# A list scheduler without program order between two readers of one tile: adaLN, an S4 convolution and a squared-ReLU FFN on one core

## The chip, the cores and the metric

The kernel runs on one core of one Trainium2 chip. The metric is the device time of one execution in microseconds (us), as the median of three runs. Five engines share the work: TensorE (PE, with its weight loads as PEld), VectorE (DVE), ScalarE (ACT), GpSimd (POOL) and SyncE (SP), which only issues transfers. The profile is of one execution, with all times counted from the start of its span.

## The reference

The input `u` is 2048 x 512, the state space model has 128 complex states for each of the 512 channels, the feed-forward part goes from 512 to 1792 and back. Cut to what is computed:

```
sa, ca, ga, sb, cb, gb = (silu(c) @ w_mod) split in six
h = layernorm(u) * (1 + ca) + sa
K[d, l] = Re sum_n C[d,n] * exp(dt[d] * A[d,n] * l) * dt[d] * B[d,n]
y = causal convolution of h with K along l (by FFT of 4096) + h * Dskip
x = u + ga * y
h = layernorm(x) * (1 + cb) + sb
out = x + gb * (relu(h @ w1 + b1)**2 @ w2 + b2)
```

## The kernel before

The kernel has four stages. In the head the parameters of the state space model are worked out (`parameters`, two calls: one for the first block of 64 channels, instructions of 128 x 64, one for the other seven, 128 x 7 x 64, lines 486 to 537), the modulation vectors (L579) are turned into a scale and a shift for every row (L611 to L616), and 16 rows of 128 positions are scaled (DVE L626 and L627), transposed by matmuls (PE L631, into two PSUM banks in turn) and copied (ACT L634).

The middle stage makes the convolution. Channels go in eight blocks `c` of 64. Each block passes through two matmul stages of a transform, stage 1 (PE L668, copied by ACT L670) and stage 2 (PE L678, copied by ACT L701), and a transfer that swaps its halves (L708). The transform of K is made in 32 units `u` of 16 channels, four to a block. For one unit POOL multiplies out amplitudes (L780, L784) from tables of exponentials (L754), and adds up the phases as integers (L736 for a block, L760 for a unit); ACT takes sine, absolute value and cosine (L770 to L772); DVE makes four products (L794 to L797); PE sums over the states (`kg`, L804), which ACT and DVE bring to the buffer `ksb` (L870, L871) for stage 1. K with a number means the L804 group of that unit, so K29 is the thirtieth. DVE multiplies the two spectra (L814), PE makes the first step of the inverse (L823), DVE copies it (L829).

The end of the convolution begins to load the feed-forward weights: w1 (L936) and w2 (L962) arrive in `work`, and ACT (L918) and DVE (L919) split each value into a high and a low part. A spread of gb (L912), the table `i2c` of the last inverse step (its transfer L903) and the rows of x once more (L907) belong here. Then come the second inverse step (PE L1009), the second layer norm (L1016 to L1046) and the FFN (L1083 to L1087 and L1125 to L1127), with the stores of the output.

What sets the order: all instructions are traced in program order, and then `keep_order` makes groups of them, finds for each group the groups that must come before it, and goes through them as a list scheduler, with one queue for each engine. Durations come from `weight`. Of the groups that are ready on an engine, the one with the longest way to the end is taken; `urgent` adds a number to that way for a whole block of code, taken from the table `HURRY`. The string table `ORDER` sets in which unit of K's loop which piece is traced: `r` a row, `A` to `H` the transform of a block, `a` to `h` its product and inverse, `0` to `7` its swap, `x` a batch of exponentials, `l` the late modulation. Matmuls of the FFN are held in program order by `in_turn`. The engine order that results is fixed by added dependences. In `before`, a group depends on an earlier one that touches the same cells of a tile, if either writes, or if the tile is a PSUM bank, or if both run on the same engine.

Of the kernel before, what the change touches and what calls it, by code (L numbers as in the profile page):

```python
# [13 lines left out]
I32 = mybir.dt.int32  # L14
# [23 lines left out]
NU = 32  # L38
EXPS = [(0, 1), (1, 1), (2, 2), (4, 2), (6, 2)]
ORDER = (  # L40
    "rrrrrrrrxrrrrrrrrABAA.CAAABABA.ClB.CBBCC0xC.BaaBCaaaaa.a.D..1bCDDbDbbE.E"
    "b2bE..DDExEbb.cDcccc.DE.F.FcE.c3EcFdxddFFdGF.dGdG..dd4.FeFeGee.HHeH.eH5G"
    ".e.HeGffGfHf.GH.ffH..6f.fgggg..g.gg7hhhhg"
).split(".")
HURRY = (-5134, -11930, -6, -54444, 14765, -82, 97968, -2, -603, 233, 1864, 6642, -284, 13749, 1407, -107, 6332, 4392, -789, 6471, 2150, -1844, 36197, -951, 83, -77, 1508, -2294, 89, -1791, -139, -157, 2431, -579, 674, -2630, -13726, -38198, -1676, -5575, -55525, 18242, 558, -2589, 11726, 2336, -215, -10792, 64542, -107, 672, 3536, -676, -860, 25428, 5010)
PIECES = "ABCDEFGHabcdefghl"


# [63 lines left out]
def weight(ins):  # L112

    out = ins.outs[0] if ins.outs and hasattr(ins.outs[0], "bass_ap") else None
    n = free_size(out) if out is not None else 1
    if "DMA" in type(ins).__name__:
        inside = not any("Dram" in type(a.bass_ap.tensor).__name__.title() for a in (*ins.ins, *ins.outs))
        return 60, n * out.ap[0][1] * 4 / (145 if inside else 330)
    match str(ins.engine).split(".")[-1]:
        case "PE":  # L120
            if len(ins.ins) < 2:
                return 10, 10
            cols, moving = free_size(ins.ins[1]), free_size(ins.ins[0])
# [12 lines left out]
            if n == 1:  # L136
                t = 200
            elif len(operands(ins.ins)) > 1:
                t += 95 if n > 128 else 140
            elif n <= 128:  # L140
                t += 26
            elif type(ins).__name__ == "InstTensorCopy" and n < 1024:
                t -= 40
        case "DVE":
            t = 70 + 1.04 * (free_size(ins.ins[0]) if type(ins).__name__ == "InstBNStats" else n)
            if n <= 4:
                t = 110
            elif len(operands(ins.ins)) > 2:
                t += 60
            elif type(ins).__name__ == "InstReciprocal":  # L150
                t = 70 + 6.3 * n
        case "Pool":
            t = 250 + 1.72 * n
        case _:
            t = 30
    return t, t + 65


def keep_order(tc, traced, slots, in_turn, whole, urgent):
# [40 lines left out]
    for g, il in enumerate(groups):  # L200
        for ins in il:
            for write, aps in ((False, ins.ins), (True, ins.outs)):
                for a in aps:
                    if getattr(a, "bass_ap", None) is None or "Dram" in type(a.bass_ap.tensor).__name__.title():
                        continue
                    name, rows, cells = region(a)
                    bank = name[:2] in ("ps", "tg", "kg")
                    slot = slots.get(name, name)
                    if slot in held and held[slot] != name:
                        left_by[name] = {x[0] for x in seen.get(held[slot], ())}  # L210
                    held[slot] = name
# [109 lines left out]
def tile_adaln_ssm_ffn(  # L321
# [18 lines left out]
    nc = tc.nc  # L340
# [220 lines left out]

    for c, n in ((1, 7),):
        mark = len(nc.cur_bb.bb.instructions)
        for _ in parameters(c, n):
            pass
        hurry(mark, HURRY[2])


    sl = ctile("sl", [P, 4])
# [53 lines left out]
    def row_pieces():  # L623
        for s, row in enumerate(rows):
            mark = len(nc.cur_bb.bb.instructions)
            nc.vector.scalar_tensor_tensor(row, row, mv1[:, s, 0:1], g1, op0=ALU.subtract, op1=ALU.mult)  # L626
            nc.vector.scalar_tensor_tensor(row, row, mv1[:, s, 1:2], s1, op0=ALU.mult, op1=ALU.add)  # L627
            ps = free_banks[s % 2]
            for g in range(4):
                for q in range(4):  # L630
                    nc.tensor.matmul(  # L631
                        ps[32 * q : 32 * q + 32, 128 * g : 128 * g + 128], ident[:, 32 * g : 32 * g + 32],
                        row[:, 128 * q : 128 * q + 128], start=True, stop=True)
            nc.scalar.copy(xj[:, :, 4 * s : 4 * s + 4], ps.rearrange("p (g d) -> p d g", g=4))  # L634
# [237 lines left out]
        stage1(ksb, xks[c], 4 * (u % 4))  # L872

    next(work["x"])
    for u in range(AHEAD):
        kgen_ahead(u)
    for u in range(NU + 1):
        mark = len(nc.cur_bb.bb.instructions)
        if u > 0:
            finish(u - 1)  # L880
            hurry(mark, HURRY[24 + (u - 1) // 4])
        mark = len(nc.cur_bb.bb.instructions)
        if u < NU:
            rl = kgen_amp(u)
            sn = kgen_sin(ph[u])
            kgen_ahead(u + AHEAD)
            kgen_rl(rl, *sn)
# [430 lines left out]
```

## Time and profile before

| | |
|---|---|
| median of three runs | 625.35 us (623.92 to 628.96) |
| the profiled execution, its own time | 626.78 us |
| its span | 625.0 us |
| mean granted TensorE clock | 0.986 |

The page's second part cuts the span in 40 slices of 15.6 us; each digit is the busy share of a slice in tenths.

```profile
PE   1338898999999999988899999999999999999996
DVE  4989967698789879886799998646999976655744
```

PE is full from the fifth slice on, apart from the slices around 300 us.

### The profile page before, as it was taken

How to read it: one execution, taken by the hardware profiler on the slowest of the kernel's cores; microseconds unless marked ns; L12 is line 12 of the kernel's file. 1: busy time of each engine (PE TensorE's matmuls, PEld its weight loads, DVE VectorE, ACT ScalarE, POOL GpSimd, SP SyncE). 2: the span in 40 equal slices, each digit the busy share in tenths (PEclk: the TensorE clock that was granted, in tenths of full speed). 3: DMA queues.
4: the chain of work that ended last, by engine and by line, in shares of the span. 5: the costliest groups of instructions: out<-in, count | busy, mean ns of one | idle time of the engine just before them, and what ended most of it. 6: DMA issues, size and time to landing. Idle time of an engine off the chain costs nothing.

```text
span 625.0 us, 21063 instructions
## 1 busy us (share of the span) xinstructions
PE 567.2 (91%) x9230; PEld 490.6 (78%) x9230; DVE 492.7 (79%) x874; ACT 423.9 (68%) x748; POOL 220.3 (35%) x188
## 2 busy tenths in 40 slices
PE   1338898999999999988899999999999999999996
PEld 1236888899999999988678777888888878888885
DVE  4989967698789879886799998646999976655744
ACT  2956878989988688650386876657666666666530
POOL 4859699899988979500000000000000000000000
PEclk9998999999999999998799999999999999999999
DMA  9940230230303202086006421112521622111432
GB/s 315 402 147 2 71 70 16 60 71 3 67 9 72 63 12 66 19 223 227 5 3 212 160 68 34 35 34 85 186 84 49 187 85 74 45 34 35 146 95 79
DMA packets 31211, 57.00 MB, mean 91 GB/s; under 512 B 4496, under 2 KB 13584, under 8 KB 29840
## 3 DMA queue, kind: packets, MB, share of 16 engines
q1 hardware_dynamic: 30688, 55.53, 29.4%
q8 instruction: 72, 1.18, 0.8%
q10 hardware_dynamic: 432, 0.14, 0.1%
q14 instruction: 19, 0.16, 0.1%
HBM read 43.07 MB, written 4.19 MB: 76 GB/s over the span
## 4 chain that ended last, share of the span: by engine, by line
PE 63%; DVE 17%; ACT 11%; issue 4%; DMA 3%; POOL 2%; SPq 0%; DVEq 0%; ACTq 0%; POOLq 0%
PE ps L678 8%; PE ps L668 8%; PE ps L823 7%; PE kg L804 4%; PE ps L1083 3%; PE ps L1087 3%; PE ps L1085 3%; PE tg L1125 3%; PE tg L1127 3%; PE tg L1126 3%; ACT tables L751 2%; DMA work<-w 2%; PE tg L1009 2%; PE ps L1127 2%; PE ps L1125 2%
## 5 line engine op out<-in xcount | busy, mean ns | idle before, releaser
L678 PE MATMUL ps<-xy,t_sb 128*64 128x64 f32 x2048 | 67.2, 224 | 4.1 <-DVE xy L814 1.9
L678 PEld LDWEIGHTS ps<-xy,t_sb 128*64 128x64 f32 x2048 | 64.2, 139 | 6.0 <-DVE xy L814 2.1
L919 DVE TENSOR_TENSOR w2t<-rw,w2t 128x512 fp32r<-128x512 f32 x53 | 36.3, 689 | 38.7 <-ACT w2t L918 38.5
L823 PE MATMUL ps<-e_sb,xy 128*64 128x128 f32 x1024 | 62.4, 277 | 0.7 <-DVE xy L814 0.7
L918 ACT CAST w2t<-rw 128x512 fp32r<-128x512 f32 x53 | 32.8, 618 | 44.2 <-PE kg L1127 23.8
L1070 ACT ACTIVATE more<-more,b1c 128x512 f32<-128x512 f32 x54 | 38.9, 721 | 32.4 <-DVE more L1113 17.0
L823 PEld LDWEIGHTS ps<-e_sb,xy 128*64 128x64 f32 x1024 | 57.8, 141 | 1.7 <-DVE xy L814 0.9
L1125 PE MATMUL tg<-w2t,t2t 128*128 128x512 f32 x112 | 43.9, 392 | 0.0
L670 ACT COPY xy<-ps 128x512 f32<-128x512 f32 x64 | 36.4, 592 | 11.0 <-PE ps L668 8.2
L1126 PE MATMUL tg<-w2t,t2t 128*128 128x512 f32 x112 | 43.6, 389 | 0.0
L1127 PE MATMUL tg<-w2t,t2t 128*128 128x512 f32 x112 | 43.6, 389 | 0.0
L814 DVE TENSOR_TENSOR xy<-ps,xy 128x512 f32<-128x512 f32 x64 | 39.9, 682 | 1.5 <-PE ps L678 1.5
L1083 PE MATMUL ps<-opt,wset 128*128 128x512 f32 x84 | 34.0, 405 | 2.8 <-ACT more L1094 2.8
L760 POOL TENSOR_TENSOR llph<-lo,big 128x1024 int32<-128x1024 int32 x16 | 34.3, 2144 | 5.8 <-ACT tg L772 5.8
L760 POOL TENSOR_TENSOR rtlph<-lo,big 128x1024 int32<-128x1024 int32 x16 | 34.3, 2142 | 3.0 <-ACT tg L772 2.4
L668 PE MATMUL ps<-d_sb,ksb 128*64 128x128 f32 x512 | 34.1, 276 | 0.6 <-issue 0.2
L668 PE MATMUL ps<-d_sb,big 128*64 128x128 f32 x512 | 32.9, 274 | 0.7 <-ACT big L634 0.7
L1125 PE MATMUL ps<-w2t,t2t 128*128 128x512 f32 x84 | 33.4, 398 | 0.0
L829 DVE COPY big<-ps 128x256 f32<-128x256 f32 x64 | 24.1, 417 | 11.8 <-PE ps L823 11.7
L1085 PE MATMUL ps<-opt,wset 128*128 128x512 f32 x84 | 32.9, 392 | 0.0
L1127 PE MATMUL ps<-w2t,t2t 128*128 128x512 f32 x84 | 32.8, 391 | 0.0
L1126 PE MATMUL ps<-w2t,t2t 128*128 128x512 f32 x84 | 32.7, 390 | 0.0
(265 smaller groups left out, 1594.1 us busy)
## 6 DMA issues: line engine op xcount, KB each, us to landing
rw<-w SPq DMA_DIRECT2D x53, 256.0 KB, 2.6
xy<-xy SPq DMA_DIRECT2D x16, 512.0 KB, 6.4
xy<-xt SPq DMA_DIRECT2D x24, 256.0 KB, 5.0
xy<-w_mod SPq DMA_DIRECT2D x6, 1024.0 KB, 8.4
work<-w SPq DMA_DIRECT2D x12, 512.0 KB, 4.4
out_dram<-more SPq DMA_DIRECT2D x14, 256.0 KB, 2.1
t_sb<-c_t SPq DMA_DIRECT2D x1, 2048.0 KB, 16.3
i2c<-c_i SPq DMA_DIRECT2D x1, 2048.0 KB, 8.2
```

The lines of the kernel that those rows point to most:

```text
L668: nc.tensor.matmul(ps[64 * r : 64 * r + 64, 128 * i : 128 * i + 128], src[:, i], d1_sb[:, r], start=True, stop=True)
L670: nc.scalar.copy(dst[:, o // 4], ps.rearrange("p (t m) -> p m t", t=4))
L678: nc.tensor.matmul(ps[64 * r : 64 * r + 64, 64 * i : 64 * i + 64].rearrange("p (h q t) -> p q h t", h=2, t=2), t2_sb[:, 8 * g + i, r], src ...
L760: nc.gpsimd.tensor_tensor(ph.rearrange("p d r (a b) -> p (d r) a b", a=4), bc(low_phase[:, us].rearrange("p d r b -> p (d r) b"), 2, 4), b ...
L814: nc.vector.tensor_mul(product_piece(y, g), ps, piece(x, g))
L823: nc.tensor.matmul(ps[64 * m : 64 * m + 64, 128 * i : 128 * i + 128], pairs(y)[:, g, i // 2, 64 * m : 64 * m + 64, i % 2], e1_sb[:, h], st ...
L1070: nc.scalar.activation(c, c if src is None else src, AF.Relu, bias=b1c[:, t : t + 1])
L1083: pe.append(nc.tensor.matmul(ps, dst[:, 0, wi, kt], o[:, 0, kt], start=start and kt == 0, stop=False, skip_group_check=on))
L1085: pe.append(nc.tensor.matmul(ps, dst[:, 1, wi, kt], o[:, 0, kt], start=False, stop=False, skip_group_check=on))
L1125: nc.tensor.matmul(to[m], l[:, xs], hi_, start=(t == 0), stop=False),
L1126: nc.tensor.matmul(to[m], h[:, xs], lo_, start=False, stop=False),
L1127: nc.tensor.matmul(to[m], h[:, xs], hi_, start=False, stop=(t == NF - 1))])
```

## The change

The dependence between two groups that only read the same cells of a tile on the same engine is dropped: such readers may now pass one another. The durations in `weight` are set anew for the matmuls of 64 and 32 columns, for DVE and for POOL. `ORDER` is another string, and `HURRY` has 109 numbers for 56: each row piece has its own, the three parts of each `parameters` call are told apart, and a unit of K is cut into amplitudes, sine, next phase and products, each with a number of its own for the first units. The instructions are the same 7254 in both kernels; only the order on the engines differs, and which buffer of a ring a piece gets. Lines behind 880 are up to nine further down after the change (L912 is L921, L918 is L927, L1009 is L1018).

```
 HURRY: 56 numbers -> 109 numbers; ORDER: 33 new strings
-            t = max(1.7 * moving / tiles, 116 / tiles)
+            t = 61 if moving == cols == 64 else 33 if cols == 32 and moving == 64 else max(1.76 * moving / tiles, 116 / tiles)
-            t = 70 + 1.04 * (free_size(ins.ins[0]) if type(ins).__name__ == "InstBNStats" else n)
+            t = 85 + 1.04 * (free_size(ins.ins[0]) if type(ins).__name__ == "InstBNStats" else n)
-            t = 250 + 1.72 * n
+            t = (360 if out is not None and out.bass_ap.dtype == I32 else 220) + 1.72 * n
...
-                        if h != g and (write or w or bank or of[h][0] == of[g][0]) and rows & r and cells & c:
+                        if h != g and (write or w or bank) and rows & r and cells & c:
...
-    for _ in parameters(0, 1):
-        pass
-    hurry(mark, HURRY[0])
+    for i, _ in enumerate(parameters(0, 1)):
+        hurry(mark, HURRY[(0, 56, 57)[i]])
+        mark = len(nc.cur_bb.bb.instructions)
...
-            hurry(mark, HURRY[4])
+            hurry(mark, HURRY[60 + s])
...
+    at_unit = lambda u, k: HURRY[32 + min(u, 31) // 4 if u > 5 else 84 + 4 * u + k]
...
-            hurry(mark, HURRY[24 + (u - 1) // 4])
+            hurry(mark, HURRY[24 + (u - 1) // 4 if u > 4 else 79 + u])
...
             rl = kgen_amp(u)
+            hurry(mark, at_unit(u, 0))
+            mark = len(nc.cur_bb.bb.instructions)
             sn = kgen_sin(ph[u])
+            hurry(mark, at_unit(u, 1))
+            mark = len(nc.cur_bb.bb.instructions)
             kgen_ahead(u + AHEAD)
+            hurry(mark, at_unit(u + 1, 2))
+            mark = len(nc.cur_bb.bb.instructions)
             kgen_rl(rl, *sn)
             kq[u] = rl
-            hurry(mark, HURRY[32 + u // 4])
+            hurry(mark, at_unit(u, 3))
```

The order on the engines at three places follows; a row is a line, an operation, its output and inputs with their buffer numbers, the output's shape, and how many follow in a row.

POOL, in the head, before: from the first phase of block 0 (L736) to the first two phase products of units (L760).

```order
L736 TENSOR_TENSOR lo_375<-big0_83,lo_375 128x128
L526 TENSOR_TENSOR big0_83<-big0_83 128x64
L534 TENSOR_TENSOR big0_83<-big0_83 128x64
L530 TENSOR_TENSOR big0_83<-big0_83 128x64
L527 TENSOR_TENSOR big0_83<-big0_83 128x64
L528 TENSOR_TENSOR big0_83<-big0_83 128x64
L736 TENSOR_TENSOR lo_375<-lo_375,big0_83 128x128x2 x3
L530 TENSOR_TENSOR big0_83<-big0_83 128x128 x3
L760 TENSOR_TENSOR rtlph_374<-lo_375,big0_83 128x1024
L760 TENSOR_TENSOR llph_373<-lo_375,big0_83 128x1024
```

POOL after, the same place.

```order
L736 TENSOR_TENSOR lo_375<-big0_83,lo_375 128x128
L534 TENSOR_TENSOR big0_83<-big0_83 128x7x64
L534 TENSOR_TENSOR big0_83<-big0_83 128x64
L530 TENSOR_TENSOR big0_83<-big0_83 128x64
L526 TENSOR_TENSOR big0_83<-big0_83 128x64
L527 TENSOR_TENSOR big0_83<-big0_83 128x64
L528 TENSOR_TENSOR big0_83<-big0_83 128x64
L754 TENSOR_TENSOR tables0_370<-tables0_370,big0_83 128x64x4
L736 TENSOR_TENSOR lo_375<-lo_375,big0_83 128x128x2
L530 TENSOR_TENSOR big0_83<-big0_83 128x128 x3
L784 TENSOR_TENSOR rtlph_374<-tables0_370 128x16x64
L736 TENSOR_TENSOR lo_375<-lo_375,big0_83 128x128x2 x2
```

The first L760 comes right behind these rows now; a parameter step of the other seven blocks (L534), one part of the tables (L754) and one amplitude product (L784) stand ahead of it that stood behind.

DVE, in the head, before: the spread of scale and shift (`g`, `s`), then the row scalings, L626 and L627 in turn.

```order
L613 TENSOR_TENSOR s4_350<-ps1_151,gs4_348 128x128
L531 TENSOR_SCALAR big0_83<-big0_83 128x128 x3
L626 SCALAR_TENSOR_TENSOR xy0_91<-xy0_91,mv1_71,kg0_351 128x512 x3
L627 SCALAR_TENSOR_TENSOR xy0_91<-xy0_91,mv1_71,ps0_150 128x512 x3
L626 SCALAR_TENSOR_TENSOR xy0_91<-xy0_91,mv1_71,kg0_351 128x512
L627 SCALAR_TENSOR_TENSOR xy0_91<-xy0_91,mv1_71,ps0_150 128x512
L626 SCALAR_TENSOR_TENSOR xy1_92<-xy1_92,mv1_71,kg0_351 128x512
L627 SCALAR_TENSOR_TENSOR xy1_92<-xy1_92,mv1_71,ps0_150 128x512
```

DVE after, from the last parameter steps to the last row scaling.

```order
L626 SCALAR_TENSOR_TENSOR xy0_91<-xy0_91,mv1_71,kg0_351 128x512 x3
L627 SCALAR_TENSOR_TENSOR xy0_91<-xy0_91,mv1_71,ps0_150 128x512
L531 TENSOR_SCALAR big0_83<-big0_83 128x128 x3
L627 SCALAR_TENSOR_TENSOR xy0_91<-xy0_91,mv1_71,ps0_150 128x512 x2
L626 SCALAR_TENSOR_TENSOR xy0_91<-xy0_91,mv1_71,kg0_351 128x512
L626 SCALAR_TENSOR_TENSOR xy1_92<-xy1_92,mv1_71,kg0_351 128x512 x4
L626 SCALAR_TENSOR_TENSOR xy2_93<-xy2_93,mv1_71,kg0_351 128x512 x3
L627 SCALAR_TENSOR_TENSOR xy0_91<-xy0_91,mv1_71,ps0_150 128x512
L627 SCALAR_TENSOR_TENSOR xy1_92<-xy1_92,mv1_71,ps0_150 128x512 x4
L627 SCALAR_TENSOR_TENSOR xy2_93<-xy2_93,mv1_71,ps0_150 128x512 x3
L626 SCALAR_TENSOR_TENSOR xy2_93<-xy2_93,mv1_71,kg0_351 128x512
L626 SCALAR_TENSOR_TENSOR xy3_94<-xy3_94,mv1_71,kg0_351 128x512 x4
```

Five L627 close the rows behind this. The scalings stand in runs of three, eight and five of a kind, where two kinds took turns.

ACT, at the end of the convolution, before: the last copies of K's spectrum (L870) among stage 1 copies (L670) and the first casts of the weights (L918).

```order
L870 COPY ksb0_824<-kg0_351 128x256
L918 CAST wset0_4554<-work_4557 128x512
L918 CAST wset0_4554<-work_4557 128x256
L670 COPY xy4_95<-ps1_151 128x512
L918 CAST wset1_4555<-work_4557 128x512
L670 COPY xy4_95<-ps2_152 128x512
L918 CAST wset1_4555<-work_4557 128x256
L918 CAST w2t_4556<-work_4557 128x512 x2
L870 COPY ksb1_825<-kg0_351 128x256
L918 CAST wset0_4554<-work_4557 128x1024
```

ACT after, the same place.

```order
L670 COPY xy2_93<-ps1_151 128x512
L927 CAST wset0_4554<-work_4557 128x512
L927 CAST wset0_4554<-work_4557 128x256
L870 COPY ksb0_842<-kg0_351 128x256
L927 CAST wset1_4555<-work_4557 128x512
L927 CAST wset1_4555<-work_4557 128x256
L927 CAST w2t_4556<-work_4557 128x512
L870 COPY ksb1_843<-kg0_351 128x256
L927 CAST w2t_4556<-work_4557 128x512
L670 COPY xy2_93<-ps2_152 128x512
```

The last L870 has moved ahead of one cast, and two stage 1 copies that stood between the casts are now around them.

On PE the second-stage groups (L678) that stand ahead of K29 number 57 where they were 58, with 61 groups of stage 1 and 24 of the inverse (L823) in both.

More of the change, by code (lines that the diff above doesn't have):

```diff
@@ L40 @@
 ORDER = (
-    "rrrrrrrrxrrrrrrrrABAA.CAAABABA.ClB.CBBCC0xC.BaaBCaaaaa.a.D..1bCDDbDbbE.E"
-    "b2bE..DDExEbb.cDcccc.DE.F.FcE.c3EcFdxddFFdGF.dGdG..dd4.FeFeGee.HHeH.eH5G"
-    ".e.HeGffGfHf.GH.ffH..6f.fgggg..g.gg7hhhhg"
+    "rrrrrrrrrrrrrrrrxABAABA.AACCABA.lB.0BCB.aCaaBaaBaa.DCC.D1xaC..bbCDbbbE.D"
+    "EDDE2.EbE.b.bccccD.xFcE.D.3x.cFccdEddFdd.GdFE.FdG.4dFF.eeee.HHeGF.eGHGG5"
+    "eH.eHHH.fffGf..f.GH..ff6fg.ggg.g7g.hghghh"
 ).split(".")
-HURRY = (-5134, -11930, -6, -54444, 14765, -82, 97968, -2, -603, 233, 1864, 6642, -284, 13749, 1407, -107, 6332, 4392, -789, 6471, 2150, -1844, 36197, -951, 83, -77, 1508, -2294, 89, -1791, -139, -157, 2431, -579, 674, -2630, -13726, -38198, -1676, -5575, -55525, 18242, 558, -2589, 11726, 2336, -215, -10792, 64542, -107, 672, 3536, -676, -860, 25428, 5010)
+HURRY = (-5437, -836, -664, 34241, 11, 137, 30857, 12931, 14409, 15212, 748, 6672, -3399, 3361, 710, -14, 10606, 764, 11292, 1543, 7014, 6080, 91476, -9339, 7445, 60221, 6258, 1582, 1, -7986, 157, -1482, -14996, 45, -203, -9972, -10340, -22107, -8, -21716, 104312, 10069, -2314, -43262, 11912, -15960, -7167, 4402, 144320, -1155, 4086, -508, 3386, -2956, 36466, -3806, -9978, 200038, 253629, 1942, 200083, 100083, 60019, -2925, 100022, 100064, 3661, 200081, 195822, 39964, 110339, 92, 200016, 100051, 3044, 3024, 14, 137899, -8521, -9998, -30018, 30000, -10018, 97589, -2970, 3028, -1929, -172, -66964, -5239, -6460, -31053, 10115, -59967, 200094, 60071, 5, -99983, -99903, -9951, 7786, 52753, 100034, -15336, 22, -99989, 486, 248)
 PIECES = "ABCDEFGHabcdefghl"
@@ L563, in tile_adaln_ssm_ffn @@
         mark = len(nc.cur_bb.bb.instructions)
-        for _ in parameters(c, n):
-            pass
-        hurry(mark, HURRY[2])
+        for i, _ in enumerate(parameters(c, n)):
+            hurry(mark, HURRY[(2, 58, 59)[i]])
+            mark = len(nc.cur_bb.bb.instructions)
     sl = ctile("sl", [P, 4])
@@ L874, in tile_adaln_ssm_ffn @@
     next(work["x"])
+    at_unit = lambda u, k: HURRY[32 + min(u, 31) // 4 if u > 5 else 84 + 4 * u + k]
+    mark = len(nc.cur_bb.bb.instructions)
     for u in range(AHEAD):
         kgen_ahead(u)
+    hurry(mark, at_unit(0, 2))
     for u in range(NU + 1):
@@ L884, in tile_adaln_ssm_ffn @@
             rl = kgen_amp(u)
+            hurry(mark, at_unit(u, 0))
+            mark = len(nc.cur_bb.bb.instructions)
             sn = kgen_sin(ph[u])
+            hurry(mark, at_unit(u, 1))
+            mark = len(nc.cur_bb.bb.instructions)
             kgen_ahead(u + AHEAD)
+            hurry(mark, at_unit(u + 1, 2))
+            mark = len(nc.cur_bb.bb.instructions)
             kgen_rl(rl, *sn)
             kq[u] = rl
-            hurry(mark, HURRY[32 + u // 4])
+            hurry(mark, at_unit(u, 3))
         mark = len(nc.cur_bb.bb.instructions)
```

## The prediction

> **What bounds the kernel now.** First the page's first part, then the windows, one for each stage (columns: stretch, length, then busy time and instruction count of PE, PEld, DVE, ACT and POOL, then PE clock, DMA share, GB/s), then the list of waits for PE.
>
> ```profile
> PE 567.2 (91%) x9230; PEld 490.6 (78%) x9230; DVE 492.7 (79%) x874; ACT 423.9 (68%) x748; POOL 220.3 (35%) x188
> 0.00:67.40 67.40, 29.20 (x632) 24.27 (x632) 54.70 (x129) 40.10 (x123) 45.38 (x63) 0.97 0.57 201
> 67.40:270.50 203.10, 199.33 (x5810) 189.00 (x5810) 170.94 (x273) 170.45 (x273) 174.35 (x124) 1.00 0.22 53
> 270.50:296.31 25.81, 21.85 (x443) 20.71 (x442) 18.18 (x40) 7.83 (x13) 0.58 (x1) 0.93 0.68 213
> 296.31:333.20 36.89, 32.95 (x1097) 26.13 (x1098) 32.34 (x70) 23.47 (x42) 0.00 (x0) 0.86 0.05 10
> 333.20:620.00 286.80, 283.89 (x1252) 230.46 (x1250) 214.47 (x361) 182.07 (x300) 0.00 (x0) 1.00 0.29 91
> ...
> PE ps L579 <- DMA xy<-w_mod: 13.1, 3, 11.2
> PE kg L616 <- DVE g L612: 10.8, 1, 10.8
> PE ps L631 <- DVE xy L627: 2.9, 6, 1.1
> ```
>
> PE is at work 91% of the span, and what it lacks lies almost wholly in the head: 38.2 of the first 67.4 us. Behind it PE idles 3.8 us in the middle stage, 4.0 in the end of the convolution, 3.9 in the change of stage, 2.9 in the feed-forward part. The change removes no instruction, so apart from the head a better order can win at most the sum of these, 14.6 us, and whatever PE loses inside busy time while it waits between matmuls. The feed-forward matmuls are held in program order in both kernels, and there PE is idle 1% of the time: I count **0** for that stage. Its first stretch can move by what the casts of w1 bring it sooner or later: -2 to +1.5, about the idle time that is there.
>
> **The head.** The chain of waits (start, length, what) runs over DVE's row scalings, two for each of 16 rows, then the last row's transposes on PE and its copy on ACT.
>
> ```profile
> 42.74 0.81 DVE xy L626 x2
> ...
> 44.80 1.98 DVE xy L627 x3
> 46.78 0.67 DVE xy L626
> ...
> 48.22 0.67 DVE xy L626
> ...
> 64.77 0.76 DVE xy L627
> 65.66 1.11 PE ps L631 x32
> 66.80 0.60 ACT big L634
> 67.44 2.84 PE ps L668 x48
> 70.28 1.05 PE kg L804 x64
> ```
>
> Alternating, a row costs 48.22 - 46.78 = 1.44 us on DVE; three of one kind in a row take 1.98, or 0.66 each. After the change the 32 scalings stand in batches of 3, 8 and 5. At 0.66 each that is 21.1, with some 0.6 for the changes of kind 21.7, against 65.53 - 42.74 = 22.8 now: **-1.1** on DVE. The three L531 that precede them now stand inside them, while the start no longer waits for the spread of the scale: start between 40.7 and 42.0, DVE's end at 63.2 to 64.5. But the last five L627 now come in one run, 0.66 apart, where PE needs 1.1 a row and so ends about 2.8 us after DVE, not 1.25 as now. PE's last transpose then falls at 66.0 to 67.3, the last copy at 66.6 to 67.9: between -0.8 and +0.5.
>
> Against that stands POOL, whose rows are moved past one another (start, length, engine, line, tiles; the last row is ACT's).
>
> ```profile
> 40.98 2.26 POOL L736 TENSOR_TENSOR lo<-lo,big 128x256 int32<-128x256 int32 x3 [0.41 <-DVE big L531]
> 43.19 1.53 POOL L530 TENSOR_TENSOR big<-big 128x128 int32<-128x128 int32 x3
> 44.79 2.14 POOL L760 TENSOR_TENSOR rtlph<-lo,big 128x1024 int32<-128x1024 int32 x1
> ...
> 48.98 1.16 POOL L534 TENSOR_TENSOR big<-big 128x448 int32<-128x448 int32 x1
> ...
> 56.96 1.87 POOL L754 TENSOR_TENSOR tables<-tables,big 128x256 f32<-128x256 f32 x3
> 58.91 1.96 POOL L784 TENSOR_TENSOR rtl<-tables 128x1024 f32<-128x1024 f32 x1
> ...
> 48.21 1.06 ACT L771 ACTIVATE rtlph<-rtlph 128x1024 f32<-128x1024 int32 x1
> ```
>
> The first phase product of unit 0 (L760) starts now at 44.79. In the new order one L534 (1.16), one L754 (1.87 / 3 = 0.62) and one L784 (1.96) come ahead of it: +3.74. That L534 is also put ahead of five short pieces that now fill POOL's wait for DVE, so up to 1.1 more. L760 then starts at 48.5 to 49.6 and ends at about 51.8. Unit 0's sine, absolute value and cosine (ACT L770 to L772, 3 x 1.06) follow at 51.9 to 55.1, and in the new ACT order they stand behind the third row copy: all later copies queue behind them. Two PSUM banks take the rows, so PE stops at the sixth row until 55.1. From there eleven rows at 1.1 give 67.2, the copy 67.8. So the two paths end almost together, at 66.6 to 68.3. I take 68.2, the later end, since ACT's queue is a certainty of the order and DVE's gain is not needed before it. K unit 0 (1.05 on PE) now stands ahead of the three L668 groups and lies in that gap, which gives about 1 back: **0**, between -1.5 and +3.
>
> A clock loss lies there as well.
>
> ```profile
> 48.00:50.00 2.00, 0.59 (x24) 0.32 (x17) 1.97 (x4) 1.97 (x4) 2.00 (x2) 1.00 0.04 8
> 50.00:52.00 2.00, 1.55 (x48) 1.23 (x44) 1.93 (x4) 1.76 (x3) 1.92 (x3) 0.83 0.00 0
> 52.00:54.00 2.00, 2.00 (x44) 1.85 (x40) 1.97 (x4) 0.59 (x1) 2.00 (x2) 0.50 0.00 0
> 54.00:56.00 2.00, 2.00 (x67) 1.83 (x63) 1.97 (x3) 0.72 (x2) 1.92 (x3) 0.82 0.03 8
> 56.00:58.00 2.00, 2.00 (x82) 1.84 (x75) 1.93 (x4) 1.39 (x3) 1.92 (x3) 1.00 0.00 0
> ```
>
> Already now, after a stretch with 0.59 us of work in 2, PE runs at 0.50 for a while: 48 + 44 + 67 = 159 matmuls in 6 us, where three stretches at 82 would hold 246, some 2.1 us of PE time. Now DVE's pace hides that. After the change PE is the later one there, and the same loss would show: it is in the +3. The Trainium skill ("TensorE: Matmul & The Clock Gate", part 1) says that the clock halves after an idle window of about 3.4 us and comes back after about 3.4 us of steady work; by that, an estimate, the longer gap costs some 1.7 us, so the head would end at +1.7 rather than 0. The trace agrees in the half rate (0.50), yet shows it after a gap that was not wholly idle.
>
> **The middle stage.** K29 (an L804 group) starts the end of the convolution, as it frees the buffer for w1.
>
> ```profile
> 259.47 2.02 PE ps L678 x64
> ...
> 262.36 1.11 PE kg L804 x64
> ...
> POOL rtl L780 <- PE kg L804: 7.5, 3, 6.1
> ```
>
> Up to K29 the new order has 57 second-stage groups for 58, with as many of the first stage (61) and of the inverse (24). At 2.02 / 2 = 1.0 each that is **-1.0**. POOL makes the phases and has 174.35 busy in this stage, PE 199.33, so POOL's later start by 4 to 5 us could follow through; but the moved L534, L754 and L784 are then already done, which gives 3.7 back, and POOL has 28.7 us of slack: 0. From the span of 194.9 us up to K29 (67.44 to 262.36) I take PE's groups at the prices of uninterrupted rows and find about 187, so some 8 us are lost between matmuls. The new order can halve this or make it half as large again: -4 to +4. For readers of one tile that no longer wait for one another, and with POOL's 7.5 us of waits for K units in sight, I take **-1**.
>
> **The end of the convolution.**
>
> ```profile
> 263.55 0.38 SPq L936
> ...
> 265.60 8.61 DMA work<-w
> ...
> 274.76 0.38 ACT ksb L870
> ...
> 281.12 1.81 DVE xy L814 x3
> ...
> 296.31 1.78 PE tg L1009 x88
> ...
> 278.12 0.33 SPq L903 DMA_DIRECT2D i2c<-c_i x1
> ...
> i2c<-c_i SPq DMA_DIRECT2D x1, 2048.0 KB, 8.2
> ```
>
> From K29 to the inverse DFT (L1009) pass 296.31 - 262.36 = 33.95 us. This stretch hangs on a transfer, not on PE: w1 is issued as soon as K29 has read its buffer, lands 10.7 us after the first issue (274.21), and ACT's last spectrum copy L870 is queued behind the casts of it; DVE's products L814 follow. In the new order K31 comes earlier, ahead of its PE work, but that L870 still stands behind five casts (six now), and DVE still has some 9 to 12 us of weight sums and copies ahead of the first product: **0**, -1 to +1. Were the last spectrum copy free of the transfer, it would be -2 to -4. The i2c load now stands behind four x reloads, whose buffers PE must have read; today it has 296.31 - 278.12 - 8.2 = 10 us to spare, so 0. The first normalisation of the next stage is later by one DVE group, the second 1.6 us earlier: **0**, -2 to +2.
>
> **Sum.** 0 - 1.0 - 1.0 + 0 + 0 = -2.0 on the profiled execution of 626.78 us (its span of 625.0 and 1.78 around it): 624.8. That execution stands 1.43 above the median of the three runs (625.35), so I forecast 624.8 - 1.43, or **623.3 us**. With the terms' ends mixed: 619.5 to 627.
>
> **Rivals.** One: *the change does not reach the path.* Same 7254 instructions, PE at 91%, transfers fixed; PE's order hardly matters. Then 625.3. Against it: 8 us of lost time and 14.6 of idle time behind the head that depend on order alone.
>
> Two: *the lost time shrinks by much.* If the freed order takes half of the 8 us (-4), the L678 group counts (-1) and the end of the convolution slips free of the transfer (-3), the time is 626.78 - 8 - 1.43 = 617.3. For it speaks that the new durations price the 64-column matmuls apart from the 32-column ones; against it, that POOL and the transfer keep their lengths.
>
> Three, the slower side: *unit 0's late phase.* L760 is 4.8 us late; if the whole K chain runs as late as this (POOL cannot catch up as its next products wait for K units) and the half clock's 2.1 us come on top, it is 626.78 + 4.8 + 2.1 - 1.43 = 632.2. It decides from the point at which the row copies end after 71 instead of 68.2, for then neither K0's place nor DVE's gain covers it. Against it speak POOL's 28.7 us of slack in the middle.
>
> **Chances.** Forecast 0.45, rival one 0.20, rival two 0.26, rival three 0.09. A measurement of this kernel can tell about 1% from no change: faster is below 619.1, slower above 631.6. Rival two lies below but for its weaker cases (0.22 of 0.26), and 0.03 of the forecast's tail joins it: 0.25. Rival three gives 0.06 and the unknown waits of i2c and w1 0.01: 0.07. The rest, 0.68, is within 1%. The range reaches down to 616, into rival two, and up to 629.5, where half of rival three's price is paid; 0.1 is left out at either end.
>
> **What would show it.** Right: the last row copy at 67 to 69, a PE gap near 50 to 55 with a clock of 0.50 behind it, L1009's replacement about 34 us after K29, and K29 near 260.5 to 262. Wrong: K29 below 257 (rival two), or a span K29 to the inverse below 31; last copy above 71 (rival three); i2c landing last ahead of the inverse.

## The result: slower by one per cent

| | before | after |
|---|---|---|
| median | 625.51 us (623.92 to 628.96, 4 runs) | 632.18 us (631.60 to 635.00, 4 runs) |
| profiled execution | 626.78 us | 631.98 us |
| its span | 625.0 us | 629.8 us |

The ratio is 1.0101, 95% interval 1.0057 to 1.0145; a second set of runs of the same kernel gave 1.0098 (1.0068 to 1.0128). The forecast was 623.3 us, range 616 to 629.5. In one later kernel, the one with the normalisation brought back, two of the seven runs were disturbed (668 and 1949 us) and are left out of its median.

The page's first part and the windows of the kernel after, cut at its own events (first stage-1 group, K31, first inverse DFT group, then 340 us in the feed-forward part). Columns are as in the prediction.

```profile
PE 568.1 (90%) x9230; PEld 491.2 (78%) x9230; DVE 492.4 (78%) x874; ACT 425.1 (67%) x748; POOL 220.1 (35%) x188
0.00:65.85 65.85, 31.77 (x696) 27.78 (x696) 57.75 (x133) 41.27 (x124) 45.75 (x64) 0.95 0.58 206
65.85:273.28 207.43, 197.07 (x5704) 185.29 (x5700) 165.43 (x265) 169.78 (x271) 174.16 (x124) 1.00 0.22 51
273.28:298.98 25.70, 22.79 (x488) 21.48 (x489) 20.33 (x44) 7.99 (x13) 0.18 (x1) 1.00 0.71 223
298.98:340.00 41.02, 35.40 (x1107) 27.89 (x1108) 33.23 (x71) 25.44 (x44) 0.00 (x0) 0.92 0.09 21
340.00:625.00 285.00, 281.06 (x1242) 228.73 (x1240) 213.73 (x361) 180.56 (x298) 0.00 (x0) 1.00 0.29 89
```

The work is the same (PE 568.1 us busy for 567.2), but the middle stage now has 10.4 us in which PE does nothing, where it had 3.8. The chain of waits dates the stages: the row copies, K0, the first stage-1 group, K29, the load of w1, the last spectrum copy, the products, the first inverse DFT group.

```profile
53.47 0.52 ACT big L634
...
54.03 10.97 PE ps L631 x352
65.00 0.92 PE kg L804 x62
65.92 1.89 PE ps L668 x30
...
265.89 1.11 PE kg L804 x64
...
267.07 4.65 DMA work<-w
...
272.66 0.28 ACT ksb L870
...
284.95 4.89 DVE xy L814 x8
...
298.98 1.77 PE tg L1018 x88
```

Against before (start of the stage's first matmul):

| | before | after | difference | in this stage alone |
|---|---|---|---|---|
| work of the middle begins (L668 before, K0 after) | 67.44 | 64.79 | -2.65 | -2.65 |
| K29 | 262.29 | 265.82 | +3.53 | +6.18 |
| inverse DFT | 296.31 | 298.98 | +2.67 | -0.86 |
| first FFN matmul | 317.32 | 321.59 | +4.27 | +1.60 |
| end of the span | 625.0 | 629.8 | +4.8 | +0.6 |

The other 0.4 us of the 5.2 between the two profiled executions lie outside the span. So the head gained, and the middle stage lost more than twice of that. To see how, I took the start times of PE's matmuls and subtracted from each interval the pace of an uninterrupted row (54.7 ns for L668 and L823, 29.1 for L678, 16.4 for L804). What is left over 0.2 us is a wait if it stands between two groups of matmuls, and a stop if it stands inside a group. Up to K29:

| kernel | waits between groups | stops inside a group | K29 |
|---|---|---|---|
| before | 3.2 | 2.4 | 262.3 |
| after | 10.1 | 4.0 | 265.8 |
| after, second profile | 9.4 | 4.7 | 267.2 |

The waits have grown by 7 us and come again; the stops have grown by 1.6 to 2.3 us. The lists of PE's waits in this stretch, first of after, then of before, name who releases them ("issue" is time in which the engine waited for nothing that the profile shows).

```profile
PE ps L823 <- ACT xy L701: 1.9, 2, 1.0
PE ps L678 <- issue: 1.5, 1, 1.5
PE ps L668 <- ACT xy L670: 1.2, 3, 0.6
PE ps L823 <- issue: 0.9, 2, 0.7
PE kg L804 <- DVE rtlph L797: 0.6, 1, 0.6
...
PE ps L668 <- DVE ksb L871: 0.5, 1, 0.5
PE ps L678 <- ACT xy L670: 0.4, 1, 0.4
PE ps L823 <- ACT xy L670: 0.3, 1, 0.3
```

```profile
PE ps L678 <- issue: 1.7, 1, 1.7
PE ps L823 <- DVE xy L814: 0.7, 1, 0.7
...
PE kg L804 <- DVE ksb L871: 0.3, 1, 0.3
PE ps L678 <- ACT xy L670: 0.2, 1, 0.2
```

After, PE waits for ACT's copies out of PSUM (L670, L701, and by way of `ksb` L870); before, it hardly does. The timeline (start, length, engine, line, tiles, idle time before and its releaser) shows one such wait of after: 24 exponentials and a table load stand ahead of a copy on ACT, and PE's next group needs the bank that the copy empties.

```profile
158.22 1.28 ACT L751 ACT_TABLE_LOAD   x1
159.52 5.82 ACT L751 ACTIVATE tables<-big 128x128 f32<-128x128 f32 x24
165.13 0.63 ACT L701 COPY xy<-ps 128x512 f32<-128x512 f32 x1
...
165.82 1.97 PE L823 MATMUL ps<-e_sb,xy 128*64 128x128 f32 x32 [0.84 <-ACT xy L701]
```

ACT is full in both kernels between 110 and 130 us; the windows show before first, then after. What differs is PE: 19.4 of 20 us busy before, 17.7 after. By the matmuls counted in the trace, PE ran four groups of L823, which DVE copies, and three of L668, which ACT copies, between K5 and K7 before (107.5 to 120.7 us); between K6 and K7 after (109.1 to 121.5) it ran two of L823 and six that ACT has to copy.

```profile
110.00:120.00 10.00, 10.00 (x230) 9.74 (x228) 6.47 (x14) 9.96 (x30) 7.48 (x7) 1.00 0.35 80
120.00:130.00 10.00, 9.42 (x298) 8.52 (x294) 8.65 (x14) 9.97 (x16) 10.00 (x7) 1.00 0.01 3
```

```profile
110.00:120.00 10.00, 8.70 (x192) 8.06 (x180) 4.69 (x9) 9.94 (x22) 5.93 (x6) 1.00 0.09 20
120.00:130.00 10.00, 9.00 (x312) 8.07 (x310) 8.27 (x12) 10.00 (x15) 7.96 (x6) 1.00 0.01 3
```

### The profile page after: what moved, and what is told of

Same layout as the page of the kernel before. It is cut to its first block, busy times and chain, and to the rows that moved or that the text cites. A ratio compares the mean times of both kernels' runs of the same rounds, so it can differ in the third digit from the quotient of the medians.

```text
span 629.8 us, 21062 instructions
## 1 busy us (share of the span) xinstructions
PE 568.1 (90%) x9230; PEld 491.2 (78%) x9230; DVE 492.4 (78%) x874; ACT 425.1 (67%) x748; POOL 220.1 (35%) x188
## 4 chain that ended last, share of the span: by engine, by line
PE 59%; DVE 14%; ACT 11%; POOL 6%; issue 5%; DMA 3%; DVEq 0%; ACTq 0%; POOLq 0%; SPq 0%
PE ps L823 6%; PE ps L668 5%; PE ps L678 4%; PE ps L1092 4%; PE ps L1094 4%; PE ps L1096 4%; PE tg L1134 3%; PE ps L1136 3%; PE ps L1134 3%; PE ps L1135 3%; PE tg L1136 3%; PE tg L1135 3%; PE kg L804 3%; DVE xy L814 3%; PE ps L631 2%
## 5 line engine op out<-in xcount | busy, mean ns | idle before, releaser
L678 PE MATMUL ps<-xy,t_sb 128*64 128x64 f32 x2048 | 66.8, 223 | 2.5 <-issue 1.5
L678 PEld LDWEIGHTS ps<-xy,t_sb 128*64 128x64 f32 x2048 | 64.0, 138 | 4.3 <-ACT xy L670 1.6
L823 PE MATMUL ps<-e_sb,xy 128*64 128x128 f32 x1024 | 61.9, 275 | 3.6 <-ACT xy L701 1.9
L927 ACT CAST w2t<-rw 128x512 fp32r<-128x512 f32 x53 | 32.8, 619 | 43.4 <-PE kg L1136 20.9
L823 PEld LDWEIGHTS ps<-e_sb,xy 128*64 128x64 f32 x1024 | 55.9, 139 | 6.4 <-ACT xy L701 2.3
L670 ACT COPY xy<-ps 128x512 f32<-128x512 f32 x64 | 36.7, 588 | 14.9 <-PE ps L668 14.8
L668 PE MATMUL ps<-d_sb,ksb 128*64 128x128 f32 x512 | 33.9, 275 | 3.5 <-issue 1.5
L760 POOL TENSOR_TENSOR rtlph<-lo,big 128x1024 int32<-128x1024 int32 x16 | 34.3, 2142 | 4.8 <-ACT tg L772 4.3
L760 POOL TENSOR_TENSOR llph<-lo,big 128x1024 int32<-128x1024 int32 x16 | 34.3, 2146 | 3.9 <-ACT tg L772 3.9
L668 PE MATMUL ps<-d_sb,big 128*64 128x128 f32 x512 | 33.3, 275 | 0.6 <-issue 0.2
```

Of the source, the lines that this page charges most:

```text
L668: nc.tensor.matmul(ps[64 * r : 64 * r + 64, 128 * i : 128 * i + 128], src[:, i], d1_sb[:, r], start=True, stop=True)
L670: nc.scalar.copy(dst[:, o // 4], ps.rearrange("p (t m) -> p m t", t=4))
L678: nc.tensor.matmul(ps[64 * r : 64 * r + 64, 64 * i : 64 * i + 64].rearrange("p (h q t) -> p q h t", h=2, t=2), t2_sb[:, 8 * g + i, r], src ...
L760: nc.gpsimd.tensor_tensor(ph.rearrange("p d r (a b) -> p (d r) a b", a=4), bc(low_phase[:, us].rearrange("p d r b -> p (d r) b"), 2, 4), b ...
L823: nc.tensor.matmul(ps[64 * m : 64 * m + 64, 128 * i : 128 * i + 128], pairs(y)[:, g, i // 2, 64 * m : 64 * m + 64, i % 2], e1_sb[:, h], st ...
```

## The experiments

The theory: the order that the new tables make for the middle stage has PE stand behind ACT's copies ("theory ACT"). Rivals: POOL's later phases; the new rule by itself; the tables being good for one rule and one set of durations only.

**The head alone.** In the kernel before, the first places of each engine's list are filled in the order that after has there; all that follows keeps the order of before.

```diff
...
-        for ins in groups[g]:
+        lists.setdefault(e, []).append(g)
+    for e, order in lists.items():
+        head = HEAD.get(e, ())
+        order[: len(head)] = [order[i] for i in head]
+        for g in order:
...
```

> The kernel before, with only the head of each engine's order (up to the last row copy, with the first K unit) taken from the kernel after; all behind it in the order of before. If the loss of the changed kernel lies in its middle stage, this keeps the head's gain (first K unit at 64.8 us and first stage-1 group at 65.9, for 70.2 and 67.4) and has no loss behind it: K29 near 259.5 to 260.5 (before 262.3, after 265.8) and 622 to 624 us, 1.5 to 3.5 below before. If the late first phase product and the half clock in the head are what costs (the slower rival of the prediction), K29 comes at 264 or later and the time is at 627 or above.

Measured: K0 at 64.73, the first stage-1 group at 65.78, K29 at 260.5, waits up to K29 4.2 us; 624.07 us, ratio to before 0.9982 (0.9949 to 1.0015). The stages came as expected, so the loss lies in the order behind the head: with the head of after and the order of before behind it, the waits are 4.2 us and the time is 8 us below after. The gain of 1.8 us at K29 on before is too small to be told from no change in the time.

**ACT relieved.** The same edit in both kernels: it leaves out the absolute value of 896 of 1024 columns, and takes the cosine of half the phase instead. One more line, in `weight`, keeps the planner's duration for the shortened instruction, and so each kernel keeps its own order.

```diff
...
-        nc.scalar.activation(flat_(ab), flat_(ph), AF.Abs)
-        last_sin[0] = nc.scalar.activation(flat_(cs), flat_(ab), AF.Sin, scale=-TWO_PI / TURN, bias=halfpi)
+        nc.scalar.activation(flat_(ab)[:, 0:128], flat_(ph)[:, 0:128], AF.Abs)
+        last_sin[0] = nc.scalar.activation(flat_(cs), flat_(ph), AF.Sin, scale=-0.5 * TWO_PI / TURN, bias=halfpi)
```

> The kernel after in its own order, but ACT's absolute value (L771) covers 128 of 1024 columns, and the cosine reads the phase itself with half the scale: the absolute value is left out for the rest, some 0.87 us of ACT less in each of 32 units. Theory ACT (PE waits in the middle stage for copies that stand on ACT behind sines and exponentials): the time lost on PE up to K29 falls from 19 to about 13, K29 at 258 to 261. Rival POOL (the phases of POOL come late): K29 moves by less than 2 us, 264 or later.

> The same relief of ACT in the kernel before and its order. Theory ACT: before, PE has other work while ACT is full, so it gains less than the kernel after: K29 from 262.3 to 259 to 261.5, a gain of 1 to 3 where the kernel after gains 5 to 8. If ACT's load is paid by both orders alike, both gain the same.

> The kernel of the second experiment once more (absolute value over 128 of 1024 columns, cosine of half the phase, order of after), now timed: its profile had one 1.9 us stop of PE in the middle of a K unit that no other run showed there. Theory ACT: without that stop the time lost on PE up to K29 is near 13.5 us and K29 near 260.3, for 19.0 and 265.8 in the kernel after; the time 626 to 629. If the stop comes again it belongs to the kernel, and K29 is again at 262.

> The kernel of the third experiment once more, timed (same part left out, order of before). K29 at 262 to 263 as in the first look, so no gain from the relief of ACT; the time 626 to 631, depending on PE's stops between K31 and the inverse DFT, which took 28.6 us there for 25.8 in the kernel before. If those stops are chance, that stretch comes back to 26.

Measured, each kernel twice:

| relieved kernel | waits up to K29 | stops up to K29 | K29 | time |
|---|---|---|---|---|
| after, first | 5.8 | 3.8 | 262.2 | 629.62 (one run) |
| after, second | 5.4 | 8.3 | 267.7 | 630.95 (629.58 to 632.97) |
| before, first | 3.2 | 4.0 | 262.6 | 630.65 (one run) |
| before, second | 2.5 | 4.8 | 262.8 | 624.85 (622.12 to 628.14) |

The waits of after fell by 4.3 and 4.7 us (by 3.6 and 4.0 from its second profile), those of before by nothing and by 0.7. That is what theory ACT says of the waits, and it accounts for about three fifths to two thirds of their growth; 2.6 to 2.9 us more than in the relieved kernel before stay. No wait for POOL stands in the lists of after, and one of 0.5 us in that of the second relieved profile. The list of PE's waits in the first relieved after kernel (lines one further down) has no stage-1 wait for an ACT copy left:

```profile
PE kg L805 <- issue: 1.7, 1, 1.7
PE ps L824 <- ACT xy L702: 1.0, 1, 1.0
PE ps L679 <- issue: 0.9, 1, 0.9
```

What I expected of K29 and of the times was missed. K29 was to come at 258 to 261 and came at 262.2, as PE stopped 1.9 us inside K10; from there to the inverse DFT the same profile took 2.2 us longer than after (35.4 for 33.2), with a stop of 2.8 us in it. The second profile, of an execution of 632.97 us, was to be free of the stop inside K10 and had it again, with a longer one at 68 us ahead of it. The stop inside K10 does not come from the relief: the unchanged kernel after has it in its second profile too (1.8 us).

ACT's busy time fell by 21.6 us in after (425.1 to 403.5) and by 20.5 in before (423.9 to 403.4). The kernel after came out 1.2 us lower (630.95 for 632.18; ratio to before 1.0087, 1.0057 to 1.0118), and so did the kernel before (624.85 for 626.06, the median of before beside it; ratio 0.9975, 0.9949 to 1.0002). Neither gain is clear of the noise. The two relieved kernels are 6.1 us apart, where the unrelieved ones are 6.7. So most of the added waits are shown to hang on ACT's load, but the lost time is not: the times fit the rival, that both orders gain the same, and what keeps the relieved kernel after slower stays open. The first run of the relieved kernel before took 630.65 us, as PE needed 28.6 us from K31 to the inverse DFT, with three stops of 1.9, 1.9 and 2.7 us; in the second profile that stretch took 24.4, so the length of those stops was chance.

**The copies moved.** In the kernel after, five ACT copies are taken ahead of what they stood behind; nothing is left out. The pairs are places in ACT's list, from and to.

```diff
+MOVES = {'Activation': ((261, 260), (226, 225), (153, 152), (115, 114), (273, 271))}
...
+    for e, order in lists.items():
+        for i, j in MOVES.get(e, ()):
+            order.insert(j, order.pop(i))
...
```

> The kernel after, with five short ACT copies for which PE waited moved ahead of the instruction they stood behind: three stage-1 copies (L670) and one copy of a K unit (L870) ahead of a sine, absolute value or cosine, and the copy of K30 ahead of the two casts that wait for w1. Nothing is left out. Theory ACT: PE's waits at these places (0.63, 0.37, 0.35, 0.51 and 1.31 us) go, K31 comes 2 to 3.5 us earlier (273.3 before the move, so 270 to 271.5), the time falls by 1 to 3 us to 629 to 631. If ACT is simply full there and the waits only pass to the next copy, K31 moves by less than 1 us.

Measured: 634.47 us, ratio to before 1.0140 (1.0108 to 1.0172), so no gain. Of the five waits two are gone, the one ahead of K31 fell from 1.50 to 0.29 us by the count above and one from 0.83 to 0.50; the fifth grew from 0.70 to 1.55, and the one behind the exponentials, not touched, from 1.06 to 2.00. Up to K29 the waits add up to 9.3, not 10.1. That would fit an ACT that is full, where a copy that goes first makes the next one late, but this profile, of an execution of 636.31 us, cannot show it: PE lost 8.1 us to stops up to K29, for 4.0 in after, 2.8 of them in a stop at 68 us that the last section shows. K31, which was to tell the two theories apart, came 4.6 us later than in after.

**The rule, the tables, the durations apart.** Three kernels: the old condition put back into after (the line is shown); the new condition alone in before, the same line the other way round; the three old lines of `weight` put back into after.

```diff
-                        if h != g and (write or w or bank) and rows & r and cells & c:
+                        if h != g and (write or w or bank or of[h][0] == of[g][0]) and rows & r and cells & c:
```

> The kernel after with two readers of one tile on one engine kept in program order again, tables and durations as after. If the rule itself loses the time, this is at or below 626. Theory tables (the new tables are made for the new rule, and the loss lies in their order, not in the rule): slower than after by over 10 us, since the order that the tables ask for is blocked by the rule, above 640.

> The kernel before with the dependence between two readers dropped and nothing else: old tables, old durations. Theory tables (a table is good only for the rule and the durations under which it was searched): slower than before by over 5 us, 631 or more. If the rule by itself frees the order, as its fewer dependences suggest, 625 or less.

> The kernel after with the durations of before in the planner, new tables and new rule kept. If the new durations hide ACT's load and so lose the middle stage, K29 comes earlier than 265.8 and the time is at 628 or less. Theory tables: the order falls apart, slower than after by over 5 us, 637 or more.

Measured, one run each: 685.07 us for after with the old rule (K0 at 82.9, waits of 44.7 us up to K29), 633.70 for before with the new rule (waits 10.4, K29 at 267.8), 637.22 for after with the old durations (waits 15.4, K29 at 270.8). Each part exchanged alone makes the order worse than in the kernel it was exchanged in. The rule, which only takes constraints away, costs the old tables 8 us, and the waits of that kernel are as long as those of after (10.4 for 10.1). So the loss cannot be put down to one of the three: the tables hold for one rule and one set of durations, and the new set of all three is not as good in the middle stage as the old one. The new tables or the new durations alone in before were not run.

**The change of stage.** In after, DVE's first L1037 goes straight behind the reciprocal, and ACT's first two L1043 ahead of the second square root.

```diff
+MOVES = {'DVE': ((457, 449),), 'Activation': ((287, 289),)}
```

> The kernel after with the first normalisation brought back to where before has it: DVE's L1037 straight behind the reciprocal instead of behind the next four L1025 and their statistics, and ACT's first two L1043 ahead of the second square root. If this later normalisation is what the change of stage lost, the first FFN matmul follows the inverse DFT by 21.0 to 21.8 us instead of 22.6, and the time falls by about 1 us, to 631. If the matmuls of L1018 hold the transposes anyway, 22.3 to 22.8 and no change.

Measured: 22.3 us from the inverse DFT to the first FFN matmul (22.6 in after, 22.1 in its second profile), so no change there. The time, 630.63 us, ratio to before 1.0083 (1.0048 to 1.0117), cannot be told from after's. The later normalisation is not what that stretch lost; it took 21.0 in before, but 22.3 in a kernel further down that has the order of before there. Of the 1.6 us a part is chance, and the rest stays open.

**POOL's phase first.** In after, one L534, one L754 and one L784 go back behind the first L760.

```diff
+MOVES = {'Pool': ((44, 47), (39, 46), (33, 45))}
```

> The kernel after with the three POOL instructions that had come ahead of the first phase product put behind it again (one L534, one L754, one L784). The prediction's step: the late phase holds ACT's row copies and so the end of the rows; then stage 1 starts 2 to 3.5 us earlier than 65.9, at 62.4 to 64. If DVE's run of eight L626 and the half clock behind it set the rows' pace, stage 1 starts at 65 to 65.9.

Measured: the timeline of PE (lines a few further down) has the row transposes in one piece behind a gap, and stage 1 at 65.28.

```profile
49.58 13.82 PE L637 MATMUL ps<-xy,ident 128*32 128x128 f32 x416 [4.72 <-DVE xy L633]
64.22 1.13 PE L810 MATMUL kg<-rtl 128*32 128x64 f32 x64 [0.83 <-DVE rtl L803]
65.28 5.48 PE L674 MATMUL ps<-d_sb,big 128*64 128x128 f32 x96
```

The phase came 2.3 us earlier (45.74 for 48.03), stage 1 only 0.6 us; the time was 630.25 us (one run). What holds the rows is DVE's run of eight L626, during which no row is finished, and behind it PE's own pace. This run also speaks against POOL's late phase as the cause of the loss in the middle stage: with the phase of unit 0 as early as this, the waits up to K29 are still 9.7 us and K29 comes at 265.7. In after, PE waits for the end of the run of eight as well:

```profile
49.98 3.64 PE L631 MATMUL ps<-xy,ident 128*32 128x128 f32 x64 [3.51 <-DVE xy L627]
```

**The head mended.** The transplanted head on the kernel before, with DVE's run of eight split in two of four, ACT's first sine group behind four more row copies, and K0 behind three stage-1 groups; then, in a second kernel, also the second unit's sine behind the last two row copies. The edit is in the numbers of `HEAD`; here are the rows that they move.

```diff
-            DVE: L626 x8, L627 x8
+            DVE: L626 x4, L627 x4, L626 x4, L627 x4
-            ACT: L770, L771, L772, L634 x4
+            ACT: L634 x4, L770, L771, L772
-            PE:  L804 x32, L668 x8 x3
+            PE:  L668 x8 x3, L804 x32
```

> The kernel before with the head of the kernel after, mended in three places: DVE scales rows 4 to 11 in two runs of four of a kind instead of one of eight, ACT takes unit 0's sine, absolute value and cosine behind four more row copies, and PE runs three stage-1 groups ahead of the first K unit. Theory: in the head of the kernel after PE stands idle for 3.5 us behind the run of eight L626 and then runs six us at half clock; with this gone the first stage-1 group starts at 63.2 to 64.2 with the clock near 1.00 from 48 to 60, K29 at 258.7 to 260, and the time is 1.5 to 4.5 us under before, 620.5 to 623.5. If DVE's length and not PE's clock sets the end of the rows, stage 1 starts at 65 or later and nothing is won over the plain transplanted head (624.1).

> The kernel before with the mended head, and in it ACT's first sine of unit 1 moved behind the last two row copies, ahead of which it stood. The first stage-1 group, which waits for the last of these copies, starts at 63.8 to 64.3 instead of 65.0, K29 at 259 to 259.6, and the time is 0.5 to 1 us below the mended head, 2 to 4 below before: 621.5 to 623.5. If the sine's delay costs the second K unit as much, K29 stays at 260.

The windows of after, then those of the mended head:

```profile
48.00:50.00 2.00, 0.02 (x3) 0.05 (x4) 2.00 (x4) 0.00 (x0) 1.97 (x1) 0.76 0.00 0
50.00:52.00 2.00, 2.00 (x40) 2.00 (x44) 2.00 (x4) 1.77 (x2) 2.00 (x2) 0.50 0.03 8
52.00:54.00 2.00, 1.62 (x32) 1.17 (x24) 2.00 (x4) 1.97 (x4) 2.00 (x3) 0.50 0.00 0
54.00:56.00 2.00, 1.97 (x40) 1.83 (x44) 2.00 (x4) 0.46 (x1) 2.00 (x2) 0.53 0.01 4
```

```profile
50.00:52.00 2.00, 1.17 (x44) 0.84 (x36) 2.00 (x4) 1.39 (x4) 2.00 (x2) 1.00 0.00 0
52.00:54.00 2.00, 1.29 (x39) 1.12 (x43) 2.00 (x4) 1.94 (x3) 2.00 (x3) 1.00 0.00 0
```

With the gap of 3.5 us cut to waits of 1.0 and 1.5 the clock stays at 1.00 and PE has time to spare. Stage 1 starts at 65.02 and in the second kernel at 64.43, K29 at 260.0 and 259.1 (262.3 before). The times are 623.29 us, ratio to before 0.9968 (0.9938 to 0.9998), and 623.04, ratio 0.9977 (0.9953 to 1.0001). The interval of the first lies below 1, if barely, and that of the second touches it; both keep the old rule for the middle stage, and neither time can be told from that of the plain transplanted head. Stage 1 was expected at 63.2 to 64.2 in the first kernel and 63.8 to 64.3 in the second: 0.8 and 0.1 us late. By its start at 65.02 the first met the rival's sign. The second shows what held 0.6 us of that: a sine that stood ahead of the last two row copies on ACT.

**After once more.**

> The kernel after, unchanged, profiled a second time. If PE's waits between its groups belong to the order, they come again at the same places: 9 to 11 us up to K29, 3 in the kernel before, and K29 at 264 to 266 where no instruction block is late. If PE stops again in the first stage-1 groups (at their 30th matmul, at 68 us), for over 2 us, the load of w_mod has pushed an instruction block back, and K29 is 3 to 5 us later than that. If the waits are chance, they fall to 6 or less.

Measured: waits of 9.4 us, stops of 4.7, K29 at 267.2, a little later than expected, as K0 came 0.8 us later and PE stopped 1.8 us inside K10; 631.95 us. The waits belong to the order. No stop at 68 us in this profile.

## Why the prediction failed, point by point

- **The head, 0 (-1.5 to +3):** wrong to the good side, -2.65 with K0 done in it. "DVE's end at 63.2 to 64.5" was 61.0, as the first scaling started at 39.0, not at 40.7 to 42. Unit 0's sine, absolute value and cosine were where "all later copies queue behind them", so that "PE stops at the sixth row": PE waited for that copy 0.41 us only, since DVE's run of eight had held the fourth row to 49.98 already. The step missed that a batch of one kind on DVE starves PE although it is faster; the half clock it foresaw came, from 50 to 56 us. The Trainium skill ("TensorE: Matmul & The Clock Gate", part 1) has the clock halve after an idle window of about 3.4 us; the trace agrees with 0.50 after a wait of 3.51, but half clock also followed a stop of 2.32, shorter than that (last section). It has the clock come back after as long a time of steady work; here it took six us, with PE at work 1.62 of 2 us in one of the windows on the way.
- **The middle stage, lost time -1 (-4 to +4):** this term failed. The stage took 6.2 us more with one second-stage group less, so the lost time grew by 7.2 us, 3 beyond the upper end. The waits between groups alone grew by 7.0. I took the sum of lost time as something that a freer order would lower, and did not ask which engine sets it. Before had ACT full at 110 to 130 us with PE hardly waiting; a new order of PE's groups there had little to win and much to lose. The relief of ACT shows three fifths to two thirds of the added waits to be ACT's, not that the time comes back with them. The -1.0 for one second-stage group less ahead of K29 was right: the trace has 57 for 58.
- **The end of the convolution, 0 (-1 to +1):** right, -0.86. w1 was still issued with the end of K29, and the last spectrum copy still came behind its casts.
- **The change of stage, 0 (-2 to +2):** +1.6, inside the bounds. The later normalisation, which I had counted, moved that stretch by 0.3 us when it was put back.
- **The feed-forward part, 0:** right within 0.6.
- **The sum** was -2.0 against the profiled execution and came to +5.2 (631.98 for 626.78). Of the signs of being wrong none came: they looked for K29 early or the row copies late, and the row copies were early and K29 late. The rest of the miss of 8.9 us is the 1.43 us that I took off because before's profiled execution stood above its median; after's stands 0.2 below its own.
- **Rival three** has the right time (632.2) by luck, for the wrong reason: the rows ended early, not after 71 us, and K5 came 4.0 us earlier than in before, so no chain of K units was late behind them. **Rival one**, that the order hardly matters, is refuted by 685 us for one condition. Rival two, lost time that shrinks, went the other way.

## What to carry to other kernels

A scheduler's tables, its dependence rule and its durations are one thing: a change in one wants a new search, and the plan that wins that search wants a run: here each exchange of one alone cost 5 to 53 us. Before you count on a freer order, look for the stretches where the second engine is full (here ACT at 9.9 of 10 us) and ask what the bound engine does there that needs nothing from it. A batch of one kind on a feeding engine saves its own time and can still starve the engine behind it.

## What the runs showed of the hardware that was not expected

PE stops inside a group at places that recur in a kernel's order, for a time that changes from run to run: inside K10, at the same matmul, for 1.2 to 2.0 us in five of the seven profiles with the order of after, and for less than 0.2 in the other two. At 68 us the stop goes with a transfer. The last of the six chunks of w_mod (1 MB) is issued at 63.5 to 65.9 us in these seven. The instruction queue's records have a 16 KB block there. In four profiles it starts 0.3 to 1.1 us ahead of the issue, and PE does not stop. In after it starts at 65.52, 0.5 us behind it; in the second relieved kernel at 67.52 and in the one with the moved copies at 67.99, 3.2 and 3.8 us behind it. PE's timeline in after and then in the second relieved kernel, with that kernel's windows:

```profile
65.85 1.96 PE L668 MATMUL ps<-d_sb,big 128*64 128x128 f32 x30
68.05 3.93 PE L668 MATMUL ps<-d_sb,big 128*64 128x128 f32 x66 [0.23 <-issue]
```

```profile
65.75 1.96 PE L669 MATMUL ps<-d_sb,big 128*64 128x128 f32 x30
70.02 5.59 PE L669 MATMUL ps<-d_sb,big 128*64 128x128 f32 x66 [2.32 <-issue]
```

```profile
66.00:68.00 2.00, 1.71 (x30) 1.46 (x26) 2.00 (x1) 1.18 (x3) 1.92 (x2) 1.00 0.94 348
68.00:70.00 2.00, 0.00 (x0) 0.00 (x0) 2.00 (x5) 0.00 (x0) 2.00 (x2) 1.00 0.42 156
70.00:72.00 2.00, 1.98 (x26) 1.98 (x28) 1.67 (x2) 0.85 (x2) 2.00 (x2) 0.70 0.05 11
72.00:74.00 2.00, 2.00 (x22) 2.00 (x20) 0.00 (x0) 0.88 (x2) 2.00 (x2) 0.50 0.00 0
```

At the same thirtieth matmul PE stops for 0.23 us or for 2.32 (2.59 with the moved copies), while the load has 0.94 of the DMA engines, and the longer stop is followed by half clock, which shows 22 matmuls in 2 us. ACT is idle in the same stretch (0.00 busy at 68 to 70), DVE and POOL are not. With the half clock the two kernels that had the long stop reached K8 at 127.7 and 129.6, after at 125.5. That a load issued ahead of the block pushes it back is read from these times; no run moved the load to try it.
